# First token tile in two halves around the second one, its half sums kept in HBM, and every engine's queue in written order

## The chip, the cores and the metric

The kernel runs on one core of a Trainium2 chip. The metric is device time in microseconds of one execution; smaller is better. Engines are named as in the profile: PE (matmul), PEld (weight load), DVE (vector), ACT (scalar), POOL (GpSimd), SP (the queue that issues the DMAs).

## The reference

Attention within chunks of 64 tokens, then a feed-forward layer with g = h cos(h), all in fp32:

```python
scores = scale * np.matmul(q_c, k_c.transpose(0, 1, 2, 4, 3))      # chunk by chunk, 64 x 64
scores = scores - np.max(scores, axis=-1, keepdims=True)
attn = np.exp(scores)
attn = attn / (np.sum(attn, axis=-1, keepdims=True) + 1e-09)
out = np.matmul(attn, v_c)
...
x = out.transpose(0, 2, 1, 3).reshape(B * S, H * D)                 # 4608 x 512
h = x @ w_in                                                        # 512 -> 2048
g = h * np.cos(h)
return (g @ w_out).astype(np.float32)                               # 2048 -> 512
```

There are 8 batches, 8 heads, 576 tokens and a head size of 64. The weights arrive as 64-bit floats, so that the kernel turns them into fp32 itself.

## The kernel before

The 4608 tokens make NT = 9 tiles of TOK = 512. The hidden width of 2048 is cut into NFC = 16 chunks of 128. A step is one chunk of one tile: `hidden(t, fc)` is 12 matmuls into a bank `h` (four slices of x, each as high x high, high x low, low x high, since every fp32 operand is split into two fp32r parts), `activate` makes g and its parts `g_hi` and `g_lo`, and `project(t, fc)` is 12 matmuls that add to four banks `acc`, one for each 128 tokens (`sub`). `project` runs LAG = 3 steps behind `hidden`. After a tile's last chunk `finish` copies the four sums out and stores them.

`activate` alternates two engines: ACT L353 (multiples of 2 pi), DVE L354 (the remainder), ACT L356 (sine), DVE L357 (times h), ACT L360 (`g_hi`), DVE L361 (`g_lo`).

A weight block (`in` or `out`, 32 in all, 512 KB each) is decoded by `split_weight`: ACT L124 (Abs), L125 (Relu) and L126 build words of the fp32 number, DVE L127 adds the sign and L130 joins the words (called xor below), ACT L136 makes the high part and DVE L137 the low part. Tile 0 needs block after block; each is decoded once and kept.

Attention of a tile works on four pairs of heads (`hp`). For tiles 0 and 1 `scores_early` writes one bank per pair, `softmax` does the maximum, difference, exponential, sums, inverse and quotients (for tile 1 the quotients are one operation on POOL), `transposed` turns the weights on PE with a copy `pts` by ACT, and `weighted` multiplies with v and splits the result into the two parts of x (ACT L321, DVE L322). From tile 2 on `attend` spreads the same over the steps of the tile before, with DVE's 32x32 transposes, through small queues of closures (`soon`, `late`, `full`) that `activate` empties.

The order within an engine's queue is set by a scheduler for tile 0 and the start: `ordered` is False there, and the scheduler may move any instruction ahead of another. From tile 1 on `kept` holds the matmuls and most of the rest in written order. Blocks are decoded two steps ahead:

```python
AHEAD = 2
...
        if s + AHEAD < NFC:
            split_weight("in", s + AHEAD)
            split_weight("out", s + AHEAD)
```

Of the kernel before, what the change touches and what calls it, by code (L numbers as in the profile page):

```python
# [29 lines left out]
AHEAD = 2  # L30
# [10 lines left out]
def attention_then_cos_ffn(ctx: ExitStack, tc, qT, kT, v, w_in, w_out, out, wide):  # L41
# [17 lines left out]
    xp = ctx.enter_context(tc.tile_pool(name="xp", bufs=8))  # L59
    gp = ctx.enter_context(tc.tile_pool(name="gp", bufs=3))  # L60
    ps_o = ctx.enter_context(tc.tile_pool(name="ps_o", bufs=1, space=bass.MemoryType.PSUM))
# [15 lines left out]

    soon = deque()
    late = deque()
    full = deque()  # L80
# [30 lines left out]
    def split_weight(name, fc):  # L111

        raw, n = w_raw.pop((name, fc))
        w = dec.tile([P, n], F32, name="w")
        if not wide:
            nc.gpsimd.tensor_copy(w, raw[:, :n])
        else:
            top = raw[:, 4 : 4 + 4 * n].rearrange("p (n k) -> p n k", k=4)[:, :, 0]
            mid = raw.bitcast(U32)[:, 1 : 1 + 2 * n].rearrange("p (n k) -> p n k", k=2)[:, :, 0]


            half, low = half_words[(name == "out")], w.bitcast(U32)
            hb = half[:, :, 1]
            nc.scalar.activation(hb.bitcast(BF16), top.bitcast(BF16), AF.Abs)  # L124
            nc.scalar.activation(hb, hb, AF.Relu, bias=float(7 - (MORE << 7)), scale=8.0)  # L125
            nc.scalar.activation(low, mid, AF.Relu, bias=float((1 << 19) - 1), scale=-(2.0**-13))  # L126
            nc.vector.scalar_tensor_tensor(  # L127
                hb, top, 0x8000, hb, op0=ALU.bitwise_and, op1=ALU.bitwise_or
            )
            nc.vector.tensor_tensor(  # L130
                low, low, half.rearrange("p n k -> p (n k)").bitcast(U32), op=ALU.bitwise_xor
            )
        o = SHIFT if name == "in" else 0
        parts = wts.tile([P, 2 * n + PAD], F32R, name=f"w_{name}{fc}")
        hi, lo = parts[:, o : o + n], parts[:, o + n : o + 2 * n]
        nc.scalar.copy(out=hi, in_=w)  # L136
        nc.vector.tensor_tensor(lo, w, hi.bitcast(F32), op=ALU.subtract)  # L137
        w_parts[name, fc] = (hi, lo)
# [6 lines left out]
    probs = {}  # L145
    def load_qk(t, hp):
        qt, kt = (att.tile([P, TOK], F32, name=n, bufs=HP) for n in ("qt", "kt"))
        nc.sync.dma_start(out=qt, in_=qT[t, hp])
        nc.sync.dma_start(out=kt, in_=kT[t, hp])
        queries[t, hp] = (qt, kt)  # L150

    def load_v(t, hp):
# [3 lines left out]
        else:  # L156
            if hp == 2:
                values["roomy"] = xp.tile([P, 2, TOK], F32, name="x")
# [16 lines left out]
    def scores_early(t, hp, s):  # L175

        qt, kt = queries.pop((t, hp))
        for c in range(NCH):
# [6 lines left out]
        m = att.tile([P, NCH], F32, name="m", bufs=4)  # L185
        nc.vector.tensor_reduce(out=m, in_=sv, op=ALU.max, axis=AX.X)
        nc.vector.tensor_tensor(
            e[:, hp], sv, m.unsqueeze(2).broadcast_to([P, NCH, CH]), op=ALU.subtract
        )
# [30 lines left out]
    def softmax(t, a, b):  # L220

        n = (b - a) * NCH
        e = probs[t][:, a:b].rearrange("p a c k -> p (a c) k")
        nc.scalar.activation(e, e, AF.Exp, scale=SCALE)
        z = att.tile([P, HP * NCH], F32, name="z")
        zs = z[:, :n]
        nc.vector.tensor_reduce(out=zs, in_=e, op=ALU.add, axis=AX.X)
        nc.vector.tensor_scalar(zs, zs, 1e-9, None, op0=ALU.add)
        nc.vector.reciprocal(out=zs, in_=zs)

        eng = nc.gpsimd if t == 1 else nc.vector
        eng.tensor_tensor(e, e, zs.unsqueeze(2).broadcast_to([P, n, CH]), op=ALU.mult)

    def exponentials(t):
        e = probs[t].rearrange("p a c k -> p (a c k)")
        kept(nc.scalar.activation(e, e, AF.Exp, scale=SCALE))

    def divide(t):

        z = att.tile([P, HP, NCH], F32, name="z")  # L240

        def total(hp):
            kept(nc.vector.tensor_reduce(out=z[:, hp], in_=probs[t][:, hp], op=ALU.add, axis=AX.X))

        def inverse():
            kept(nc.vector.tensor_scalar(z, z, 1e-9, None, op0=ALU.add))
            kept(nc.vector.reciprocal(out=z, in_=z))

        def quotient(hp):
            e = probs[t][:, hp]  # L250
            zb = z[:, hp].unsqueeze(2).broadcast_to([P, NCH, CH])
            kept(nc.vector.tensor_tensor(e, e, zb, op=ALU.mult))

        soon.extend(lambda hp=hp: total(hp) for hp in range(HP))
        soon.append(inverse)
        return [lambda hp=hp: quotient(hp) for hp in range(HP)]

    def transposed(t, hp):
# [4 lines left out]
        pt = ps_h.tile([P, 512], F32, name="h") if t == 0 else bank("a", 0)  # L263
        for c in range(0, NCH, 2):
            nc.tensor.transpose(
# [3 lines left out]
            )  # L269
        nc.scalar.copy(out=pts, in_=pt)  # L270
# [19 lines left out]
    def weighted(t, hps, banks):  # L290
# [18 lines left out]
        if (t, g) not in x_parts:  # L309
            x_parts[t, g] = tuple(  # L310
                xp.tile([P, 2, TOK], F32R, name="x") for _ in range(2)
            )
        for par in range(2):
# [6 lines left out]
            def split(xq=xq, hi=hi, lo=lo):  # L320
                kept(nc.scalar.copy(out=hi, in_=xq))  # L321
                kept(nc.vector.tensor_tensor(lo, xq, hi.bitcast(F32), op=ALU.subtract))  # L322

            if t < EARLY:
                split()
            else:
                late.append(split)


    g_parts = {}  # L330
    acc = {}

    def hidden(t, fc):
        if t == 0 and fc in (2, 3):
            h = bank("a", fc)
        else:
            h = ps_h.tile([P, TOK], F32, name="h")
# [9 lines left out]
    def activate(t, fc, h):  # L347

        g = gp.tile([P, TOK], F32, name="g", bufs=2)
# [4 lines left out]
        kept(nc.vector.scalar_tensor_tensor(g, n, -2.0 * math.pi, h, op0=ALU.mult, op1=ALU.add))  # L354
        take(soon, 1)
        kept(nc.scalar.activation(g, g, AF.Sin, bias=0.5 * math.pi))  # L356
        kept(nc.vector.tensor_tensor(g, h, g, op=ALU.mult))  # L357
        take(soon, 1)
        take(full, 2)
        kept(nc.scalar.copy(out=g_hi, in_=g))  # L360
        kept(nc.vector.tensor_tensor(g_lo, g, g_hi.bitcast(F32), op=ALU.subtract))  # L361
        g_parts[t, fc] = (g_hi, g_lo)
# [3 lines left out]
    def project(t, fc):  # L366
        g_hi, g_lo = g_parts.pop((t, fc))
        w_hi, w_lo = w_parts["out", fc]
        for sub in range(NSUB):
            if fc == 0:  # L370
# [3 lines left out]
            matmul(o, g_hi[:, ss], w_hi, start=(fc == 0), stop=False)  # L374
            matmul(o, g_hi[:, ss], w_lo, start=False, stop=False)
            matmul(o, g_lo[:, ss], w_hi, start=False, stop=(fc == NFC - 1))
            if fc == NFC - 1:
                full.append(lambda sub=sub, o=o: finish(t, sub, o))

    def finish(t, sub, o):  # L380
        if t == NT - 1:
            if sub % 2 == 0:
                acc["last"] = xp.tile([P, 2, DM], F32, name="x")
            os = acc["last"][:, sub % 2]
        else:

            os = (wts if sub % 2 else dec).tile([P, DM], F32, name=f"half{sub // 2}" if sub % 2 else "w")
# [149 lines left out]
```

## Time and profile before

| | |
|---|---|
| median of 3 runs | 880.53 us (880.53 to 880.63) |
| the profiled execution | 880.95 us |
| its span, first to last instruction | 879.1 us |
| mean granted clock of PE | 0.986 |
| HBM read, written | 45.09 MB, 9.44 MB |
| DMA queue q1 | 17.7% of 16 engines |

Spans of the profile are counted from the first instruction. A group of matmuls shows its first start and its last end; the time from start to start of neighbours is what an operation costs on a queue that never waits, since its end overlaps with the next start. In brackets behind a row stands how long the engine idled ahead of it and who ended that.

### The profile page before, as it was taken

The numbers are of one execution on the slowest core, as the hardware profiler recorded it, in microseconds if no ns is written. First come the engines' busy times: TensorE is split into PE (matmuls) and PEld (weight loads), VectorE is DVE, ScalarE is ACT, GpSimd is POOL, SyncE is SP. The second block draws the span as 40 slices with busy tenths as digits, with TensorE's granted clock in tenths as the row PEclk, the third lists the DMA queues.
The fourth block names the chain that finished last, engine by engine and source line by source line (L and its number), as shares of the span: only waits on it lengthen the run. The fifth ranks groups of instructions, "written<-read, shape, count | busy, mean of one in ns | idle before, by whom it ended". The sixth has DMA issues, their size and how long they took to land.

```text
span 879.1 us, 14100 instructions
## 1 busy us (share of the span) xinstructions
PE 853.0 (97%) x5792; PEld 697.1 (79%) x5792; DVE 576.7 (66%) x975; ACT 407.9 (46%) x660; POOL 5.5 (1%) x9
## 2 busy tenths in 40 slices
PE   4899999999999999999999999999999999999998
PEld 3587777888888888888888888888888888888886
DVE  5999986766577656764686558655766577644332
ACT  4998993533354335333533344333533354333332
POOL 0001000000000000000000000000000000000000
PEclk8599999999999999999999999999999999999999
DMA  9980013100310012001300040003100010001001
GB/s 346 406 340 33 14 25 110 47 26 25 96 49 25 24 49 96 25 1 50 120 1 25 25 145 1 25 25 97 49 25 25 1 48 25 1 1 48 1 1 48
DMA packets 25407, 55.42 MB, mean 63 GB/s; under 512 B 2816, under 2 KB 2816, under 8 KB 25344
## 3 DMA queue, kind: packets, MB, share of 16 engines
q1 hardware_dynamic: 25344, 54.54, 17.7%
q8 instruction: 45, 0.74, 0.4%
q14 instruction: 18, 0.15, 0.1%
HBM read 45.09 MB, written 9.44 MB: 62 GB/s over the span
## 4 chain that ended last, share of the span: by engine, by line
PE 85%; ACT 11%; DMA 1%; DVE 1%; issue 1%; SPq 0%; ACTq 0%
PE acc L74 41%; PE h L74 40%; PE a L74 4%; ACT half L124 2%; ACT half L125 2%; ACT w L126 2%; DMA w_out<-in_w_out_dram 1%; ACT g_hi L360 1%; ACT g L356 1%; ACT w_out L136 1%; ACT w_in L136 1%; ACT g L353 1%; DMA kt<-in_kT_dram 1%; ACT pts L270 0%; ACT x L321 0%
## 5 line engine op out<-in xcount | busy, mean ns | idle before, releaser
L74 PE MATMUL h<-x,w_in 128*128 128x512 f32 x1704 | 416.9, 393 | 5.9 <-ACT x L321 2.8
L74 PEld LDWEIGHTS h<-x,w_in 128*128 128x128 f32 x1704 | 321.1, 189 | 75.0 <-DVE g L357 4.5
L74 PE MATMUL acc<-w_out,g_hi 128*128 128x512 f32 x1152 | 355.2, 392 | 0.0
L74 PEld LDWEIGHTS acc<-w_out,g_hi 128*128 128x128 f32 x1152 | 214.0, 188 | 45.2
L74 PE MATMUL acc<-w_out,g_lo 128*128 128x512 f32 x576 | 221.1, 390 | 0.6 <-DVE g_lo L361 0.6
L354 DVE SCALAR_TENSOR_TENSOR g<-g,h 128x512 f32<-128x512 int32 x142 | 97.2, 684 | 138.3 <-ACT g L353 137.6
L353 ACT ACTIVATE g<-h 128x512 int32<-128x512 f32 x142 | 84.7, 596 | 190.1 <-PE h L74 190.1
L361 DVE TENSOR_TENSOR g_lo<-g,g_hi 128x512 fp32r<-128x512 f32 x144 | 102.5, 712 | 79.9 <-ACT g_hi L360 77.0
L356 ACT ACTIVATE g<-g 128x512 f32<-128x512 f32 x144 | 91.0, 632 | 128.2 <-DVE g L354 128.0
L360 ACT CAST g_hi<-g 128x512 fp32r<-128x512 f32 x144 | 89.3, 620 | 128.9 <-DVE g L357 79.3
L357 DVE TENSOR_TENSOR g<-h,g 128x512 f32<-128x512 f32 x142 | 98.1, 691 | 56.5 <-ACT g L356 53.0
L74 PEld LDWEIGHTS acc<-w_out,g_lo 128*128 128x128 f32 x576 | 108.1, 188 | 23.7 <-DVE g_lo L361 1.1
L282 DVE STREAM_TRANSPOSE pts<-e 32x256 f32<-32x256 f32 x224 | 97.4, 435 | 3.7
L125 ACT ACTIVATE half<-half 128x512 uint16<-128x512 uint16 x32 | 25.1, 786 | 0.2
L74 PEld LDWEIGHTS a<-kt,qt 64*64 64x64 f32 x1024 | 18.9, 135 | 7.6 <-issue 6.8
L130 DVE TENSOR_TENSOR w<-w,half 128x512 uint32<-128x512 uint32 x32 | 22.0, 687 | 1.8 <-ACT w L126 1.0
L74 PEld LDWEIGHTS a<-pts,vt 64*64 64x64 f32 x1024 | 16.6, 134 | 7.2 <-issue 5.3
L322 DVE TENSOR_TENSOR x<-a,x 128x512 fp32r<-128x512 f32 (+1 forms) x38 | 21.9, 614 | 0.1
L74 PE MATMUL a<-kt,qt 64*64 64x64 f32 x1024 | 21.8, 222 | 0.0
L74 PE MATMUL a<-pts,vt 64*64 64x64 f32 x1024 | 19.0, 222 | 0.7 <-ACT pts L270 0.7
L216 DVE TENSOR_TENSOR e<-a,m 128x512 f32<-128x512 f32 x28 | 19.2, 686 | 0.5
L212 DVE TENSOR_REDUCE m<-a 128x8 f32<-128x512 f32 x28 | 19.2, 684 | 0.0
(61 smaller groups left out, 316.5 us busy)
## 6 DMA issues: line engine op xcount, KB each, us to landing
qt<-in_qT_dram SPq DMA_DIRECT2D x36, 256.0 KB, 4.0
kt<-in_kT_dram SPq DMA_DIRECT2D x36, 256.0 KB, 4.2
vt<-in_v_dram SPq DMA_DIRECT2D x34, 256.0 KB, 3.0
w_in<-in_w_in_dram SPq DMA_DIRECT2D x16, 512.0 KB, 9.1
w_out<-in_w_out_dram SPq DMA_DIRECT2D x16, 512.0 KB, 9.4
out_dram<-w SPq DMA_DIRECT2D x16, 256.0 KB, 2.1
out_dram<-half SPq DMA_DIRECT2D x16, 256.0 KB, 2.0
out_dram<-x SPq DMA_DIRECT2D x4, 256.0 KB, 2.0
```

Of the source, the lines that this page charges most:

```text
L74: kept(nc.tensor.matmul(*args, **kw))
L125: nc.scalar.activation(hb, hb, AF.Relu, bias=float(7 - (MORE << 7)), scale=8.0)
L130: nc.vector.tensor_tensor(low, low, half.rearrange("p n k -> p (n k)").bitcast(U32), op=ALU.bitwise_xor)
L212: kept(nc.vector.tensor_reduce(out=m, in_=sv, op=ALU.max, axis=AX.X))
L282: kept(nc.vector.transpose(out=dst[o : o + BL, :, qb], in_=src[i : i + BL, :, kb]))
L322: kept(nc.vector.tensor_tensor(lo, xq, hi.bitcast(F32), op=ALU.subtract))
L353: kept(nc.scalar.activation(n, h, AF.Identity, bias=0.25, scale=0.5 / math.pi))
L354: kept(nc.vector.scalar_tensor_tensor(g, n, -2.0 * math.pi, h, op0=ALU.mult, op1=ALU.add))
L356: kept(nc.scalar.activation(g, g, AF.Sin, bias=0.5 * math.pi))
L357: kept(nc.vector.tensor_tensor(g, h, g, op=ALU.mult))
L360: kept(nc.scalar.copy(out=g_hi, in_=g))
L361: kept(nc.vector.tensor_tensor(g_lo, g, g_hi.bitcast(F32), op=ALU.subtract))
```

## The change

The steps are taken in another sequence: tile 0's chunks 0 to 7 (GROUP = 8), all 16 chunks of tile 1, tile 0's chunks 8 to 15, then tiles 2 to 8 as before. At the end of the first half the four sums of tile 0 go to HBM (`partial`); they are loaded again in step 28, by `resume`, and DVE adds them to the second half's sums in step 34. Tile 1's attention, which had all 16 steps of tile 0, now has eight.

The 32 blocks are decoded over 19 steps: two at the start (`in` 0 and 1, where four were), then one or two inside each `activate` (`split_in`), for the first eight chunks two steps ahead of their use, for the others in turn until step 18. Three pieces of a block stand between the operations of the activation, so that the sequence on each engine is written out. `ordered` is gone: every instruction of ACT, DVE and PE keeps the written order from the first on. The start is written out by hand too; two of tile 0's quotients go to POOL, and tile 1's are four operations there. The buffers `xp` are half as many under two names.

```diff
+GROUP = 8
...
-    ordered = False
-
     def kept(ins):
-        if ordered:
-            tc.keep_in_program_order(ins)
+        tc.keep_in_program_order(ins)
         return ins
...
+    order = [(0, fc) for fc in range(GROUP)] + [(1, fc) for fc in range(NFC)]
+    order += [(t, fc) for t in range(NT) if t != 1 for fc in range(0 if t else GROUP, NFC)]
...
+    partial = [hbm.tile([P, DM], F32, name=f"partial{sub}") for sub in range(NSUB)]
...
-    def activate(t, fc, h):
+    left = []
+    def activate(t, fc, h, blocks=()):
+        nothing = [lambda: None] * 7
+        one, two = ([split_weight(*b) for b in blocks] + [nothing, nothing])[:2]
...
         kept(nc.scalar.activation(n, h, AF.Identity, bias=0.25, scale=0.5 / math.pi))
         kept(nc.vector.scalar_tensor_tensor(g, n, -2.0 * math.pi, h, op0=ALU.mult, op1=ALU.add))
+        for piece in left:
+            piece()
+        left.clear()
+        for piece in one[:2]:
+            piece()
         take(soon, 1)
         kept(nc.scalar.activation(g, g, AF.Sin, bias=0.5 * math.pi))
+        for piece in one[2:4]:
+            piece()
         kept(nc.vector.tensor_tensor(g, h, g, op=ALU.mult))
+        one[4]()
         take(soon, 1)
+        take(urgent, len(urgent))
         take(full, 2)
         kept(nc.scalar.copy(out=g_hi, in_=g))
+        two[0]()
         kept(nc.vector.tensor_tensor(g_lo, g, g_hi.bitcast(F32), op=ALU.subtract))
+        for piece in one[5:] + two[1:5]:
+            piece()
+        left.extend(two[5:])
...
+    def resume():
+        for sub in range(NSUB):
+            os = acc["partial", sub] = out_room(sub)
+            nc.sync.dma_start(out=os, in_=partial[sub])
...
+        if half == 0 and step in (1, 2):
+            for hp in (2 * step - 2, 2 * step - 1):
+                late.append(scores_early(t, hp, bank("a", hp)))
+        if half == 0 and step == 3:
+            late.append(lambda: exponentials(t))
+        if half == 0 and step == 4:
+            soon.extend(lambda hp=hp: total(t, hp) for hp in range(HP))
+            soon.append(lambda: inverse(t))
+            soon.extend(lambda hp=hp: quotient(t, hp, nc.gpsimd) for hp in range(HP))
+        hp = {(5, 1): 0, (6, 0): 1, (7, 0): 2, (7, 1): 3}.get((step, half))
+        if hp is not None:
+            take(late, len(late))
+            (late if hp < HP - 1 else urgent).extend(weighted(t, (hp,), (bank("a", 0), bank("a", 1))))
...
+        if (step, half) in ((5, 0), (6, 1)):
+            take(late, len(late))
+            for hp in range(2 * (step - 5), 2 * (step - 4)):
+                transposed(t, hp)
...
+    for fc in range(2, GROUP):
+        split_in.setdefault(fc - 2, []).append(("in", fc))
+    for fc in range(GROUP - 1):
+        split_in.setdefault(fc + 1, []).append(("out", fc))
+    rest = [("out", GROUP - 1)] + [(k, fc) for fc in range(GROUP, NFC) for k in ("in", "out")]
+    s = GROUP
+    while rest:
+        k = 1 + (s % 2 == 0)
+        split_in[s], rest = rest[:k], rest[k:]
+        s += 1
```

The line numbers of the operations move: L353, L354, L356, L357, L360, L361 become L370, L371, L378, L381, L386, L388; L124 to L126 become L136 to L138, L127 and L130 become L140 and L143, L136 and L137 become L150 and L155. Below, `half` names belong to decode, `a` banks to attention.

On ACT, where tile 1's first turned weights (`pts`) are copied, before:

```order
L353 ACTIVATE g<-h 128x512
L136 CAST w_out_991<-w 128x512
L124 ACTIVATE half_89<-w_out_176 128x512
L360 CAST g_hi<-g 128x512
L125 ACTIVATE half_89<-half_89 128x512
L356 ACTIVATE g<-g 128x512
L136 CAST w_in_1034<-w 128x512
L124 ACTIVATE half_87<-w_in_178 128x512
L270 COPY pts<-a_797 128x512
L126 ACTIVATE w<-w_out_176 128x512
```

and now, from the end of step 4 into step 5:

```order
L386 CAST g_hi<-g 128x512
L136 ACTIVATE half_91<-w_out_158 128x512
L150 CAST w_in_733<-w 128x512
L137 ACTIVATE half_91<-half_91 128x512
L138 ACTIVATE w<-w_out_158 128x512
L281 COPY pts<-a_763 128x512
L281 COPY pts<-a_770 128x512
L370 ACTIVATE g<-h 128x512
L150 CAST w_out_815<-w 128x512
L136 ACTIVATE half_89<-w_in_164 128x512
```

One copy among decode and the activations of two steps has become two copies ahead of everything of step 5.

On DVE, the sums and inverse of tile 1's softmax (`z`), which the quotients on POOL wait for, before:

```order
L361 TENSOR_TENSOR g_lo<-g,g_hi 128x512
L127 SCALAR_TENSOR_TENSOR half_87<-w_in_170,half_87 128x512
L228 TENSOR_SCALAR z<-z 128x32
L137 TENSOR_TENSOR w_out_908<-w,w_out_908 128x512
L357 TENSOR_TENSOR g<-h,g 128x512
L130 TENSOR_TENSOR w<-w,half_87 128x512
L229 RECIPROCAL z<-z 128x32
```

and now, in step 4:

```order
L388 TENSOR_TENSOR g_lo<-g,g_hi 128x512
L155 TENSOR_TENSOR w_in_733<-w,w_in_733 128x512
L140 SCALAR_TENSOR_TENSOR half_91<-w_out_158,half_91 128x512
L143 TENSOR_TENSOR w<-w,half_91 128x512
L257 TENSOR_REDUCE z<-e 128x8 x2
L261 TENSOR_SCALAR z<-z 128x32
L262 RECIPROCAL z<-z 128x32
L371 SCALAR_TENSOR_TENSOR g<-g,h 128x512
```

The sums, which were one operation ahead of these rows, are four in step 4, and the last two and the inverse stand behind the step's decode.

On DVE at the change from step 1 to step 2, where tile 1's scores are taken from their banks, now:

```order
L140 SCALAR_TENSOR_TENSOR half_91<-w_out_126,half_91 128x512
L143 TENSOR_TENSOR w<-w,half_91 128x512
L212 TENSOR_REDUCE m<-a_484 128x8
L214 TENSOR_TENSOR e<-a_484,m 128x512
L212 TENSOR_REDUCE m<-a_502 128x8
L214 TENSOR_TENSOR e<-a_502,m 128x512
L371 SCALAR_TENSOR_TENSOR g<-g,h 128x512
```

The four operations stand together ahead of the next step's L371, where those of the third and fourth pair were spread before:

```order
L186 TENSOR_REDUCE m<-a_602 128x8
L137 TENSOR_TENSOR w_in_847<-w,w_in_847 128x512
L130 TENSOR_TENSOR w<-w,half_89 128x512
L186 TENSOR_REDUCE m<-a_662 128x8
L357 TENSOR_TENSOR g<-h,g 128x512
L187 TENSOR_TENSOR e<-a_602,m 128x512
L127 SCALAR_TENSOR_TENSOR half_87<-w_in_166,half_87 128x512
L354 SCALAR_TENSOR_TENSOR g<-g,h 128x512
L187 TENSOR_TENSOR e<-a_662,m 128x512
```

On SP's queue four stores of `partial` come after tile 2's first v loads, and its four loads among tile 1's output stores.

More of the change, by code (lines that the diff above doesn't have):

```diff
@@ L268, in transposed @@
                 identity=ident,
[L269 to L270 removed]
+            ))
+        kept(nc.scalar.copy(out=pts, in_=pt))
         probs[t, hp] = pts
@@ L364, in activate, with project @@
             take(queue, len(queue))
-    def project(t, fc):
+    def project(s):
+        t, fc = order[s]
+        first = s == 0 or order[s - 1][0] != t
+        last = s == len(order) - 1 or order[s + 1][0] != t
         g_hi, g_lo = g_parts.pop((t, fc))
@@ new lines, in attention_then_cos_ffn @@
+        if fc == 3:
+            prefetch(1)
+    for fc in (NFC - 2, NFC - 1):
+        load_weight("out", fc)
+    blocks = [("in", fc) for fc in range(2)]
+    w0, w1 = (split_weight(*b) for b in blocks)
+    below = [scores_early(0, hp, bank("acc", hp)) for hp in range(HP)]
+    below[0]()
+    exponentials(0, 0, 1)
+    below[1]()
+    exponentials(0, 1, 2)
+    total(0, 0)
+    below[2]()
+    exponentials(0, 2, 3)
+    total(0, 1)
+    inverse(0, 0, 2)
+    quotient(0, 0, nc.gpsimd)
+    quotient(0, 1, nc.gpsimd)
@@ new lines, in attention_then_cos_ffn @@
+    w0[0]()
+    below[3]()
+    exponentials(0, 3, 4)
+    total(0, 2)
+    for piece in w0[1:5]:
+        piece()
+    total(0, 3)
+    inverse(0, 2, 4)
+    quotient(0, 2)
+    quotient(0, 3)
+    transposed(0, 0)
+    x0 = weighted(0, (0,), (bank("a", 0), bank("a", 1)))
+    transposed(0, 1)
+    x1 = weighted(0, (1,), (bank("acc", 0), bank("acc", 1)))
+    for piece in x0 + w0[5:]:
+        piece()
+    transposed(0, 2)
+    transposed(0, 3)
+    x2 = weighted(0, (2,), (bank("acc", 2), bank("acc", 3)))
```

250 lines of the change are left out of this document (125 added, 125 removed).

## The prediction

> **What bounds the kernel now.** I read the page's first block, the table by windows, the chain that ended last, then the timeline where the bound changes.
>
> ```profile
> PE 853.0 (97%) x5792; PEld 697.1 (79%) x5792; DVE 576.7 (66%) x975; ACT 407.9 (46%) x660; POOL 5.5 (1%) x9
> ```
> ```profile
> 10.00:20.00 10.00, 3.18 (x61) 2.43 (x56) 8.63 (x17) 6.73 (x12) 0.00 (x0) 0.79 1.04 409
> 20.00:30.00 10.00, 5.99 (x94) 4.10 (x90) 9.02 (x21) 9.97 (x21) 0.00 (x0) 0.50 1.04 401
> 30.00:40.00 10.00, 7.98 (x75) 5.19 (x74) 8.86 (x16) 9.97 (x20) 0.00 (x0) 0.67 1.02 406
> ...
> 100.00:110.00 10.00, 10.00 (x47) 8.09 (x46) 9.10 (x16) 10.00 (x19) 0.00 (x0) 1.00 0.01 3
> ...
> 200.00:300.00 100.00, 100.00 (x675) 82.23 (x674) 65.40 (x114) 39.38 (x62) 0.00 (x0) 1.00 0.13 43
> ```
> The columns are PE, PEld, DVE, ACT, POOL, granted clock, DMA share. From 200 us on PE is full and ACT at 39%: PE-bound. From 20 to 110 ACT is full; PE's "full" there is stretched, since far fewer matmuls fit.
>
> ```profile
> 230.26 2.95 PE acc L74 x12
> ...
> 322.58 2.95 PE acc L74 x12
> ...
> 446.37 2.72 PE h L74 x12
> ...
> 864.69 10.89 PE acc L74 x48
> ```
> Twelve matmuls, which are one `hidden` or one `project`, take 2.72 us. A tile repeats after 322.58 - 230.26 = 92.32 us; 32 x 2.72 = 87.04 of it is the feed-forward, so 5.28 is attention. PE ends at 864.69 + 10.89 = 875.58. Counting back: tiles 1 to 8 need 128 `hidden` and 131 `project` (three are left over from tile 0 by LAG), 259 x 2.72 = 704.5, and seven attentions 37.0. So tile 1 begins at 134.1, and from there nothing is lost. All that can change lies ahead of 134.1, where tile 0 is held by ACT's decode.
>
> **ACT's price list** comes from a stretch in which it never idles; what counts is start to start.
>
> ```profile
> 94.59 0.59 ACT L360 CAST g_hi<-g 128x512 fp32r<-128x512 f32 x1
> ...
> 95.09 0.59 ACT L353 ACTIVATE g<-h 128x512 int32<-128x512 f32 x1
> 95.41 0.67 DVE L361 TENSOR_TENSOR g_lo<-g,g_hi 128x512 fp32r<-128x512 f32 x1
> ...
> 95.58 0.68 ACT L126 ACTIVATE w<-w_in 128x512 uint32<-128x512 uint32 x1
> 96.01 0.67 DVE L354 SCALAR_TENSOR_TENSOR g<-g,h 128x512 f32<-128x512 int32 x1
> ...
> 96.16 0.61 ACT L136 CAST w_out<-w 128x512 fp32r<-128x512 f32 x1
> ...
> 96.67 0.80 ACT L124 ACTIVATE half<-w_out 128x512 bf16<-128x512 bf16 x1
> ...
> 97.32 0.61 ACT L356 ACTIVATE g<-g 128x512 f32<-128x512 f32 x1
> 97.83 0.79 ACT L125 ACTIVATE half<-half 128x512 uint16<-128x512 uint16 x1
> ...
> 98.47 0.62 ACT L136 CAST w_in<-w 128x512 fp32r<-128x512 f32 x1
> ...
> 99.62 0.36 ACT L321 CAST x<-a 128x256 fp32r<-128x256 f32 x1
> 99.87 0.68 ACT L126 ACTIVATE w<-w_out 128x512 uint32<-128x512 uint32 x1
> ```
> The first number of a row is its start. A decode block costs ACT 0.65 (L124) + 0.64 (L125) + 0.57 (L126) + 0.50 (L136) = 2.36; a step's activation 0.49 (L353) + 0.51 (L356) + 0.50 (L360) = 1.50; half a split of x (L321) 0.25. DVE takes 0.60 for an operation of 128x512.
>
> ```profile
> 42.57 0.83 ACT L124 ACTIVATE half<-w_in 128x512 bf16<-128x512 bf16 x1
> ...
> 43.43 0.79 ACT L125 ACTIVATE half<-half 128x512 uint16<-128x512 uint16 x1
> ...
> 70.84 1.28 ACT L224 ACT_TABLE_LOAD   x1
> ...
> 72.14 1.92 ACT L224 ACTIVATE e<-e 128x2048 f32<-128x2048 f32 x1
> ...
> 73.96 0.64 ACT L126 ACTIVATE w<-w_out 128x512 uint32<-128x512 uint32 x1
> ...
> 82.81 3.89 POOL L232 TENSOR_TENSOR e<-e,z 128x2048 f32<-128x2048 f32 x1 [80.63 <-ACT w L126]
> ...
> 133.19 0.57 ACT L270 COPY pts<-a 128x512 f32<-128x512 f32 x1
> 133.32 0.69 DVE L357 TENSOR_TENSOR g<-h,g 128x512 f32<-128x512 f32 x1 [0.70 <-ACT g L356]
> ...
> 134.05 0.62 ACT L360 CAST g_hi<-g 128x512 fp32r<-128x512 f32 x1 [0.28 <-DVE g L357]
> ```
> The first pair is Abs with its Relu right behind it: 0.86 instead of 0.65, so 0.2 is lost. A table load costs 1.30, the large exponential 1.82, one quarter of POOL's quotients 0.97. The last rows show a chain from DVE's product to `g_hi`: 0.69 and 0.04 until ACT starts.
>
> **The start.** DVE begins as now:
>
> ```profile
> 6.35 0.69 DVE L186 TENSOR_REDUCE m<-acc 128x8 f32<-128x512 f32 x1 [6.35 <-PE acc L74]
> ...
> 24.56 1.08 PE L265 MATMUL h<-ident,e 128*128 128x128 f32 x4 [1.48 <-DVE e L232]
> ...
> 27.60 1.13 PE L74 MATMUL a<-pts,x 64*64 64x64 f32 x32
> ...
> 41.58 0.62 ACT L353 ACTIVATE g<-h 128x512 int32<-128x512 f32 x1
> ```
> Its new queue up to the last quotient: four maxima and subtractions 5.3, three sums 1.8 and the last 0.6, two inversions 0.9, two operations of one decode 1.5, one quotient 0.6, and 1.6 of waits for ACT: 18.6. From there two transposes, a copy and a `weighted` at half clock, and the last halves of x behind a decode in ACT's queue, 8.8: 27.4. Six matmuls of the first `hidden` are left, at half clock 2.7, and 0.5 of latencies: it ends at 30.6. Now the first activation follows at 41.58, but with eight blocks decoded; then it will be two. The 11 us are no gain by themselves, since 6 x 2.36 = 14.2 of ACT's work is owed.
>
> **Steps 0 to 7** (tile 0's half, with all of tile 1's attention). ACT's work: 8 x 1.50 = 12.0; 13 blocks x 2.36 = 30.7; tile 1: three table loads 3.9, exponential 1.8, four `pts` copies 1.9, eight splits 2.0. Together 52.3. PE's own, 13 x 2.72 = 35.4 and some 7 of attention, lies beside it. Then the waits of a queue in written order, which I laid out row by row at the prices above:
> - g_hi stands behind Sin and only one decode operation; Sin 0.6 and the product 0.7 (begun behind L140) are not covered: 0.3 to 0.8 in seven steps, 3.7. Abs to Relu, 8 x 0.2 = 1.5. High parts that wait for DVE's xor, 1.8.
> - In steps 1 and 2 four DVE operations of tile 1's scores (4 x 0.65) stand ahead of the next step's L371, so Sin is late by 1.3 each: 2.6.
> - In step 5 two `pts` copies stand ahead of the step's first activation. They wait for the transposes, these for POOL's quotients, these for the inversion behind the last two sums on DVE. Counted from ACT's last operation of step 4: the rest of DVE's decode 1.3, two sums 1.2, inversion 0.5, quotient 0.97, transposes 0.6 make 4.6, and the second copy waits 0.5. In step 6 the other two copies wait 1.8 for `project`.
> - `hidden` 8 needs all of tile 1's x, whose last quarter is handled in step 7: 2.0.
> Sum 18.4. ACT starts at 30.7; 30.7 + 52.3 + 18.4 = 101.4, and the ninth `hidden` ends at about 101.
>
> **From there.** 135 `hidden` and 139 `project`: 274 x 2.72 = 745.3; attention 37.0. Decode goes on with 17 blocks in 11 steps: 11 x 1.50 + 17 x 2.36 = 56.6 against PE's 11 x 5.44 = 59.8, so PE leads, but with ACT and DVE about 4 us behind it, and three PE waits are left: tile 1's first `project` for the banks, whose last two copies stand behind decode, 2.5; tile 2's second pair of scores for banks that DVE empties at the end of its step (2 x 1.9 of decode and four operations, 2.4, beside 1.8 of its own), 5.8; its first `weighted` for DVE's 32x32 transposes, late after the exponential's 4.4, 2.5. Together 10.8. If LAG covers them it is nothing: that is the lower end.
>
> The parked sums (four stores, four loads of 256 KB) cost nothing: loads are issued in step 28 and used in step 34, six steps or 32 us later, and a landing takes:
>
> ```profile
> out_dram<-w SPq DMA_DIRECT2D x16, 256.0 KB, 2.1
> ```
> On SP's queue they pass only loads that are wanted steps later. Four adds on DVE in place of two copies add 1.2 where DVE is at 65%: nothing.
>
> Sum: 101 + 745.3 + 37.0 + 10.8 = 894.1. After PE's end come 879.1 - 875.6 = 3.5, around the span 880.95 - 879.1 = 1.85: 899.5 for a profiled execution, which stands 0.4 above the median: **899 us**.
>
> [...]
>
> **Rivals.**
> *ACT stays as full as now* (faster). Other work slips into every gap and the waits vanish: 30.7 + 52.3 = 83.0, then 745.3 + 37.0 + 5.3: 870. For it: ACT is at 9.97 of 10 from 20 us on. Against: there a decode operation fills each gap, in the new order the gap's next instruction is the waiting one. It decides from the point where under 11 of the 29 us of waits come. Chance 0.11.
> *The PE clock drops in the gaps.* PE gets pauses of 5 us (step 2) and 12 us (ahead of the transposes in step 5). In the trace:
>
> ```profile
> 12.50:15.00 2.50, 0.00 (x0) 0.00 (x0) 2.36 (x4) 0.51 (x2) 0.00 (x0) 1.00 1.01 407
> 15.00:17.50 2.50, 0.00 (x0) 0.00 (x0) 2.50 (x7) 1.80 (x4) 0.00 (x0) 0.67 1.02 418
> 17.50:20.00 2.50, 1.96 (x36) 1.56 (x36) 2.50 (x5) 2.50 (x5) 0.00 (x0) 0.50 1.04 402
> ```
> Without matmuls for some 5 us the clock went to 0.50. At half clock `project`, `weighted` and `hidden` between that pause and step 6 take 2.7 + 0.7 + 2.7 = 6.1 more, of which ACT's own work in step 5 covers some 2, and the `hidden` after the pause in step 2 takes 2.7 more: about 7, so 906. Chance 0.22. [...]
> *LAG covers the later waits*: 888. Chance 0.15.
> *No change that can be measured* (two thirds of the waits covered): 0.04.
> The forecast itself: 0.48, with a range of 892 to 903 of its own.
>
> **How the numbers follow.** Slower 0.48 + 0.22 + 0.15 = 0.85; same 0.04, within 0.2%, about what a measurement of this kernel can tell; faster 0.11. The range takes in the three slower cases with some room for waits missed, 882 to 911.
>
> **What would show it.** Right: the first activation near 31; ACT idle ahead of the first `pts` copies of tile 1 for about 5 us, released by PE; the ninth `hidden` ending near 101; then a PE that is full but for three waits of 2 to 6 us between 115 and 205; steps from 210 on as now. Wrong: an ACT at 9.9 of 10 from 31 to 85, or a ninth `hidden` that ends before 90.

## The result, and the profile after

The changed kernel takes 908.17 us (median; 906.77 to 909.43), the kernel before 880.58 beside it: 1.0307 times as long, with a 95% interval of 1.0285 to 1.0329. It is 3% slower, where the forecast had 2%; the forecast of 899.0 was 9.2 us too low, inside its range of 882 to 911. The profiled execution took 907.83, its span 906.1. Medians and ratios here and below are of fast runs; one run of the "sums ahead" kernel, in a slow state at 3002.38 us, is left out.

The page's engines and its row of granted clocks:

```profile
PE 859.4 (95%) x5792; PEld 701.8 (77%) x5792; DVE 579.4 (64%) x976; ACT 412.6 (46%) x660; POOL 7.7 (1%) x14
...
PEclk8887999899999999999999999999999999999999
```

The matmuls are the same; PE's share fell from 97 to 95% of a longer span, and the clock is not full in several of the first eight slices (each 22.7 us). The table by windows says where (PE, PEld, DVE, ACT, POOL, granted clock, DMA share). First the kernel before at 70 us:

```profile
70.00:80.00 10.00, 10.00 (x46) 8.29 (x45) 9.36 (x14) 9.95 (x14) 0.00 (x0) 1.00 0.00 0
```

and the changed kernel:

```profile
70.00:80.00 10.00, 4.10 (x15) 3.39 (x16) 5.21 (x10) 4.33 (x9) 4.04 (x4) 0.54 0.00 0
...
160.00:170.00 10.00, 8.27 (x81) 6.94 (x82) 6.79 (x12) 4.24 (x7) 0.00 (x0) 0.66 0.33 105
...
250.00:300.00 50.00, 50.00 (x338) 40.98 (x337) 37.01 (x64) 20.48 (x30) 0.00 (x0) 1.00 0.20 64
```

ACT, at 9.95 of 10 before, is busy 4.33 of 10 at 70 us, with PE at 4.10 and DVE at 5.21: they wait for each other. From 250 us on nothing is lost. ACT's timeline shows the waits, and PE's row behind it the longest pause:

```profile
29.56 0.59 ACT L370 ACTIVATE g<-h 128x512 int32<-128x512 f32 x1
...
46.36 0.63 ACT L378 ACTIVATE g<-g 128x512 f32<-128x512 f32 x1 [1.21 <-DVE g L371]
...
77.05 0.58 ACT L281 COPY pts<-a 128x512 f32<-128x512 f32 x1 [5.26 <-PE a L276]
...
87.98 0.65 ACT L331 CAST x<-a 128x256 fp32r<-128x256 f32 x2 [1.89 <-PE a L73]
...
91.45 1.07 ACT L281 COPY pts<-a 128x512 f32<-128x512 f32 x2 [2.82 <-PE a L276]
...
103.63 0.60 ACT L370 ACTIVATE g<-h 128x512 int32<-128x512 f32 x1 [0.84 <-PE h L73]
```
```profile
75.90 2.12 PE L276 MATMUL a<-ident,e 128*128 128x128 f32 x8 [13.38 <-POOL e L267]
```

L370, L378 and L386 are now the activation's three ACT operations (L353, L356, L360 before), L371 and L381 DVE's, L281 the copy of turned weights, L331 half a split of x, L276 the transposes. ACT's last row is the ninth activation, the first of tile 1; I call its start the ninth activation below. PE's waits behind it, and its twelves in the chain that ended last:

```profile
122.94 0.74 PE L73 MATMUL acc<-w_out,g_hi 128*128 128x512 f32 x2 [1.36 <-ACT pts L434]
124.12 0.73 PE L73 MATMUL acc<-w_out,g_hi 128*128 128x512 f32 x2 [0.21 <-DVE vt L436]
...
157.48 0.30 PE L73 MATMUL a<-kt,qt 64*64 64x64 f32 x2 [1.12 <-issue]
161.73 1.98 PE L73 MATMUL a<-kt,qt 64*64 64x64 f32 x62 [3.96 <-DVE e L243]
...
207.35 0.68 PE L73 MATMUL a<-pts,vt 64*64 64x64 f32 x28 [2.48 <-DVE pts L293]
```
```profile
163.71 4.90 PE acc L73 x12
...
208.04 4.54 PE acc L73 x12
...
302.22 2.95 PE acc L73 x12
...
394.71 2.95 PE acc L73 x12
...
891.52 10.98 PE acc L73 x48
```

The three waits are those that the prediction named. Behind the last two of them one `project` takes 4.90 and 4.54 in place of 2.72: half clock (granted 0.50 in 162 to 166 and in 210 to 212). PE ends at 902.50, against 875.58 before.

### The profile page after: what moved, and what is told of

It is laid out like the page before. It is cut to its first block, busy times and chain, and to the rows that moved or that the text cites. A ratio compares the mean times of both kernels' runs of the same rounds, so it can differ in the third digit from the quotient of the medians.

```text
span 906.1 us, 14142 instructions
## 1 busy us (share of the span) xinstructions
PE 859.4 (95%) x5792; PEld 701.8 (77%) x5792; DVE 579.4 (64%) x976; ACT 412.6 (46%) x660; POOL 7.7 (1%) x14
## 4 chain that ended last, share of the span: by engine, by line
PE 79%; ACT 11%; DVE 8%; issue 1%; DMA 1%; SPq 0%; POOL 0%; ACTq 0%; DVEq 0%; POOLq 0%
PE acc L73 39%; PE h L73 36%; PE a L73 4%; ACT half L137 2%; ACT half L136 2%; DVE half L140 2%; ACT g_hi L386 1%; DVE g L381 1%; DVE w L143 1%; ACT w_in L150 1%; ACT g L370 1%; ACT w_out L150 1%; DVE pts L293 1%; ACT g L378 1%; DMA kt<-in_kT_dram 1%
## 5 line engine op out<-in xcount | busy, mean ns | idle before, releaser
L73 PE MATMUL acc<-w_out,g_hi 128*128 128x512 f32 x1152 | 362.5, 396 | 1.6 <-ACT pts L434 1.4
L73 PE MATMUL acc<-w_out,g_lo 128*128 128x512 f32 x576 | 226.4, 393 | 0.0
L371 DVE SCALAR_TENSOR_TENSOR g<-g,h 128x512 f32<-128x512 int32 x144 | 98.6, 684 | 145.8 <-ACT g L370 145.1
L370 ACT ACTIVATE g<-h 128x512 int32<-128x512 f32 x144 | 85.8, 596 | 187.2 <-PE h L73 187.0
L388 DVE TENSOR_TENSOR g_lo<-g,g_hi 128x512 fp32r<-128x512 f32 x144 | 99.7, 693 | 81.1 <-ACT g_hi L386 76.5
L386 ACT CAST g_hi<-g 128x512 fp32r<-128x512 f32 x144 | 89.4, 621 | 136.3 <-DVE g L381 83.8
L378 ACT ACTIVATE g<-g 128x512 f32<-128x512 f32 x144 | 90.7, 630 | 128.3 <-DVE g L371 128.2
L381 DVE TENSOR_TENSOR g<-h,g 128x512 f32<-128x512 f32 x144 | 99.4, 690 | 55.0 <-ACT g L378 51.7
L73 PEld LDWEIGHTS a<-kt,qt 64*64 64x64 f32 x1024 | 20.8, 145 | 16.6 <-issue 16.6
L73 PEld LDWEIGHTS a<-pts,vt 64*64 64x64 f32 x1056 | 18.1, 137 | 13.7 <-issue 4.9
L73 PE MATMUL a<-pts,vt 64*64 64x64 f32 x1056 | 21.1, 225 | 6.4 <-DVE x L334 2.7
L137 ACT ACTIVATE half<-half 128x512 uint16<-128x512 uint16 x32 | 25.1, 783 | 0.6
L257 DVE TENSOR_REDUCE z<-e 128x8 f32<-128x512 f32 x36 | 23.7, 678 | 0.0
L143 DVE TENSOR_TENSOR w<-w,half 128x512 uint32<-128x512 uint32 x32 | 22.0, 688 | 1.3
L250 ACT ACTIVATE e<-e 128x2048 f32<-128x2048 f32 (+1 forms) x12 | 17.9, 1488 | 10.2 <-DVE e L214 10.1
```

Source lines behind the costliest of these rows:

```text
L73: kept(nc.tensor.matmul(*args, **kw))
L137: lambda: kept(nc.scalar.activation(hb, hb, AF.Relu, bias=more, scale=8.0)),
L143: lambda: kept(nc.vector.tensor_tensor(*[w().bitcast(U32)] * 2, words, op=ALU.bitwise_xor)),
L257: kept(nc.vector.tensor_reduce(out=sums[t][:, hp], in_=probs[t][:, hp], op=ALU.add, axis=AX.X))
L370: kept(nc.scalar.activation(n, h, AF.Identity, bias=0.25, scale=0.5 / math.pi))
```

## The experiments

| kernel | median us | ratio to before (95%) | ninth activation | PE end |
|---|---|---|---|---|
| changed | 908.17 | 1.0307 (1.0285 to 1.0329) | 103.63 | 902.50 |
| free order | 901.12 | 1.0219 (1.0203 to 1.0236) | 114.91 | 895.30 |
| written order, no split | 910.91 | 1.0330 (1.0312 to 1.0348) | | 904.49 |
| turned weights behind activation | 907.01 | 1.0289 (1.0268 to 1.0310) | 102.67 | 901.22 |
| tile 2's scores later | 899.25 | 1.0201 (1.0182 to 1.0221) | 103.82 | 895.66 |
| sums ahead | 904.83 | 1.0270 (1.0253 to 1.0288) | 101.50 | 898.92 |
| rewritten | 881.50 | 1.0004 (0.9995 to 1.0014) | 90.37 | 875.95 |
| rewritten, free order | 895.21 | 1.0163 (1.0148 to 1.0179) | 110.84 | 891.59 |
| rewritten, a step earlier | 882.89 | 1.0022 (1.0013 to 1.0031) | 91.34 | 876.85 |
| and `out` blocks later | 884.86 | 1.0041 (1.0027 to 1.0054) | 91.34 | 878.77 |
| quotients on DVE | 881.75 | 1.0005 (0.9997 to 1.0014) | 91.33 | 876.89 |
| and scores in steps 0, 2 | 882.31 | 1.0012 (1.0004 to 1.0021) | 91.28 | 876.82 |
| `project` first | 879.73 | 0.9987 (0.9978 to 0.9996) | 88.57 | 874.13 |

My theory was that the written order makes the loss, wait by wait; its rivals, that the split does, or that a written order costs a fixed amount per step.

**Free order.** The change, with the scheduler free until step 19:

```diff
     def kept(ins):
-        tc.keep_in_program_order(ins)
+        if ordered:                      # s >= 19
+            tc.keep_in_program_order(ins)
```

> The changed kernel, but until step 19 the scheduler may move instructions of ACT, DVE and PE, as in the kernel before; the split of tile 0, the spread of the decode and the parked sums stay. Theory (the written order makes the loss): of the roughly 21 us in which ACT waits between its first activation at 29.6 and the end of the ninth `hidden` at 103.6, most goes, since decode that is ready fills the gaps; the ninth `hidden` ends at 84 to 90, the PE pauses near 157 and 205 shrink, and the time is 870 to 885. Rival (squeezing tile 1's attention into eight steps makes the loss, whoever orders it): the chain from the last sums over POOL's quotients to the turned weights is as long as before, the ninth `hidden` ends at 98 or later, and the time stays at 900 to 910.

901.12: 7 us of 27 come back, so the theory missed. Both of the rival's numbers came (a ninth `hidden` at 98 or later, 900 to 910): tile 1's attention is what the next tile waits for here too, and its chain is longer than in the written order, not only as long (ACT's eighth and ninth activation, then windows):

```profile
89.55 0.59 ACT L373 ACTIVATE g<-h 128x512 int32<-128x512 f32 x1
114.91 0.57 ACT L373 ACTIVATE g<-h 128x512 int32<-128x512 f32 x1
```
```profile
100.00:110.00 10.00, 6.16 (x71) 4.39 (x70) 8.26 (x15) 10.00 (x21) 0.00 (x0) 0.71 0.15 56
110.00:120.00 10.00, 7.46 (x73) 5.36 (x72) 9.12 (x16) 9.97 (x19) 0.00 (x0) 0.50 0.57 173
```

Tile 0's eight steps are done by 90, earlier than in the written order, but tile 1's x is not there. ACT is full of decode that no step needs yet, and the hand-overs of tile 1's attention (`weighted`, split, turned weights, `weighted`) queue behind it. The ninth activation is 11 us later than in the changed kernel, and the spread of the decode is lost. Behind it little is lost, one PE wait of 3.47: from 114.91 to PE's end are 780.4 us, in the changed kernel 798.9.

**Written order, no split.**

```diff
-GROUP = 8
+GROUP = 16
...                # and no partial sums, no resume
```

> The written order alone: tile 0 keeps its 16 steps in one piece, two blocks are decoded in each of them, nothing is parked in HBM; every queue keeps the written order. Theory (the written order makes the loss): an ACT step is 1.50 + 2 x 2.36 = 6.2 of work and 1.2 or so of waits, so that tile 1 begins 16 to 24 us later than the 134.1 of the kernel before, and the time is 896 to 906, near the changed kernel or a little under it, since the split buys little that the waits don't take back. Rival (the split makes the loss): about 880 to 885, as before.

910.91, above the range of the theory (896 to 906): this written order costs 30 us without the split. It isn't the order alone, though. The code keeps tile 1's attention in steps 1 to 7, where sixteen steps are there for it, and PE waits 12.95 us for POOL's quotients as in the changed kernel. Behind that stand two-block steps without tile 1's attention (activations):

```profile
122.71 0.57 ACT L370 ACTIVATE g<-h 128x512 int32<-128x512 f32 x1
130.35 0.58 ACT L370 ACTIVATE g<-h 128x512 int32<-128x512 f32 x1
...
163.76 0.59 ACT L370 ACTIVATE g<-h 128x512 int32<-128x512 f32 x1
```

A step takes 7.64 for 1.50 + 2 x 2.36 = 6.22 of ACT's work; before, eight steps from 81.58 to 131.21 took 6.20 each. The seventeenth activation comes at 163.76, where the first of tile 1 came at 136.94 before. So each version loses by itself (30 us the written order without the split, 20 the split in free order), and the two together lose no more than the larger.

**Two moves of one wait.** First the copies, and with them the first two rounds of `weighted`, half a step later; then the sums:

```diff
-        hp = {(5, 1): 0, (6, 0): 1, (7, 0): 2, (7, 1): 3}.get((step, half))
+        hp = {(6, 0): 0, (6, 1): 1, (7, 0): 2, (7, 1): 3}.get((step, half))
...
-        if (step, half) in ((5, 0), (6, 1)):     # transposes and pts copies
+        if (step, half) in ((5, 2), (6, 2)):     # 2: behind the activation
```

> One wait moved: tile 1's transposes and their `pts` copies are written behind the activation of steps 5 and 6, not ahead of it, so that the 5.3 us in which ACT waits for POOL's quotients at 72 to 77 us pass beside an activation. Theory (each wait of ACT in the first eight steps is paid in full): the ninth `hidden` ends 4 to 6 us earlier and the time falls by as much, to 902 to 904. Rival (the wait only moves: the later turned weights make the later `weighted` and tile 1's x late instead): less than 1.5 us, 907 to 909.

907.01: the rival. The 5.26 us are gone, and other waits stand in their place:

```profile
78.44 0.62 ACT L386 CAST g_hi<-g 128x512 fp32r<-128x512 f32 x1 [2.13 <-PE a L276]
...
96.14 0.65 ACT L331 CAST x<-a 128x256 fp32r<-128x256 f32 x2 [4.30 <-PE a L73]
...
102.67 0.60 ACT L370 ACTIVATE g<-h 128x512 int32<-128x512 f32 x1 [1.26 <-PE h L73]
```

```diff
-            soon.extend(total ...); soon.append(inverse); soon.extend(quotient ...)
+            first.extend(total ...); first.append(inverse); first.extend(quotient ...)
     # activate(): first is emptied right behind DVE's first operation
```

> One thing moved in the changed kernel: in step 4 the four sums of tile 1, their inversion and POOL's quotients are written directly behind the first DVE operation of the activation, not spread between the decode of that step. In the changed kernel DVE idles 2.66 us ahead of that operation, and the last two sums come at 72.9 us. Theory (the sums' place sets the 5.3 us wait of ACT in step 5): the quotients start near 68 instead of 74.8, ACT's wait for the turned weights goes, and the time falls by 3 to 5, to 903 to 905. Rival (what follows, two banks handed from `weighted` to the next turned weights and back, sets the end of tile 1's attention, as moving the copies alone left the time at 907.0): ACT's wait goes and others grow in steps 6 and 7, 906 to 908.

904.83, at the upper end of the theory (903 to 905), though the trace has the rival's mechanism in it too. The copies no longer wait, step 5 begins 4.45 earlier (74.08, not 78.53), but half of that goes to the second pair:

```profile
73.60 0.59 ACT L282 COPY pts<-a 128x512 f32<-128x512 f32 x1
74.08 0.61 ACT L371 ACTIVATE g<-h 128x512 int32<-128x512 f32 x1
...
89.35 1.08 ACT L282 COPY pts<-a 128x512 f32<-128x512 f32 x2 [4.36 <-PE a L277]
```

What holds steps 5 to 7 is the chain of tile 1's attention, not one wait of it.

**Tile 2's scores later.**

```diff
-                attend(to, step)
+                if to > 2 or step == 0:
+                    attend(to, step)
+                elif step > 1:
+                    attend(to, step - 1)
```

> One PE wait moved: tile 2's second pair of scores and the attention steps behind them are issued one step later, when DVE has emptied the banks. Theory (the PE pause at 157 to 162 us is paid with the half clock behind it): 6.3 us of waiting and 2.1 of half clock go, `project` after it takes 2.72 again, and the time falls by 6 to 9, to 899 to 902. Rival 1 (LAG or DVE's queue lets PE wait elsewhere): tile 2's first `weighted` becomes later by what was won, less than 3 us in all, 905 to 908. Rival 2 (the clock drop is not tied to the pause): 6 us go, and a `project` of 4.8 stays.

899.25: 8.9 us less, the theory (PE at the same place):

```profile
159.13 2.88 PE L73 MATMUL h<-x,w_in 128*128 128x512 f32 x12
161.95 1.22 PE L73 MATMUL a<-kt,qt 64*64 64x64 f32 x64
```

The scores start without a wait, take 1.22 for 64 where the changed kernel's 62 took 1.98, and no `project` near them is stretched. The ninth activation is where it was (103.82). The wait, 5.1, and its half clock, 2.2 + 0.8, make 8.1. From the ninth activation to PE's end the trace is 7.0 shorter (798.9 became 791.8), with one new PE wait of 1.04 at 183.51; the medians differ by 8.9, between runs that spread over some 2.5 us. So the wait and its half clock were paid, nearly in full.

**Rewritten.** All at once, in written order: sums ahead; `weighted` in two rounds of two pairs; the second block's Abs ahead of `g_hi`; tile 1's maxima and differences between the decode operations; tile 2's attention later.

```diff
+        two[0]()
         kept(nc.scalar.copy(out=g_hi, in_=g))
-        two[0]()
...
-        hp = {(5, 1): 0, (6, 0): 1, (7, 0): 2, (7, 1): 3}.get((step, half))
+        if half == 1 and step in (5, 6):
+            hps = (2 * step - 10, 2 * step - 9)
+            urgent.extend(weighted(t, hps, (bank("a", 0), bank("a", 1))))
...
+    later = {0: (0,), 10: (8, 9)}      # tile 2: the other steps one later
```

> Written order throughout, five places rewritten: tile 1's sums directly behind the first DVE operation of step 4; tile 1's `weighted` in two rounds of two pairs (steps 5 and 6) in place of four rounds of one; the second block's Abs ahead of the `g_hi` copy; tile 1's maxima and differences between the decode operations, not behind them; tile 2's attention a step later from its second scores on, its first `weighted` two steps later. Theory (the loss is the waits that the written order holds, place by place): the ninth `hidden` ends near 88 to 92 instead of 103.6, the PE pauses near 157 and 205 go, and the time is 878 to 888. Rival (the written order costs a fixed amount in every step, wherever the operations stand): the first eight steps still take 8 us or more each, the ninth `hidden` ends at 97 or later, and only the two PE pauses go: 893 to 898.

881.50, the theory; the ninth activation at 90.37, 13.3 earlier, and PE ends at 875.95:

```profile
85.46 0.60 ACT L381 ACTIVATE g<-h 128x512 int32<-128x512 f32 x1
90.37 0.60 ACT L381 ACTIVATE g<-h 128x512 int32<-128x512 f32 x1 [0.18 <-PE h L73]
```

Of the 26.7 us that this wins over the changed kernel, 13.3 lie ahead of the ninth activation and 13.3 behind it (798.9 became 785.6). So the loss lay in where the rows stand, and in four rounds of `weighted` where two do. Only two of the five places were tried by themselves, the sums (3.3 us) and tile 2's attention (8.9); how the rest divides among the others is not shown.

**Rewritten, free order.** The same code with the scheduler free until step 19.

> The same code as the rewritten version, with the scheduler free to move instructions until step 19. Theory (in the free order decode that is ready goes ahead of tile 1's attention on ACT and DVE, so each hand-over of that chain costs more): ACT is full until about 120, tile 1's x is late though the chain has two rounds fewer, the ninth `hidden` ends at 103 to 112, and the time is 887 to 897, slower than the written version. Rival (the free order fills the gaps and the shorter chain is all it needed): 870 to 880, faster than the written version.

895.21, the theory; the eighth and the ninth activation:

```profile
91.75 0.59 ACT L384 ACTIVATE g<-h 128x512 int32<-128x512 f32 x1
110.84 0.60 ACT L384 ACTIVATE g<-h 128x512 int32<-128x512 f32 x1 [0.53 <-PE h L76]
```

So for the rewritten code this scheduler is 13.7 us worse than the written order, while for the changed kernel's code it was 7.1 better: neither order is the better one by itself. The 30 us by which the kernel before beats the unsplit written order are no third case, since those two differ in tile 1's attention as well.

**Four attempts to go on.** They end within 3.4 us of the rewritten version, none faster. A step earlier (`step in (0, 1)` for the scores, the rest of tile 1's attention a step earlier too, and its sums now ahead of the activation's first DVE operation):

> The rewritten version with tile 1's attention a step earlier throughout (scores in steps 0 and 1, exponential at the end of step 2, sums in step 3 ahead of that step's first DVE operation, turned weights in steps 4 and 5). Theory (in the rewritten version the ninth `hidden` waits for ACT's and DVE's work alone, whose idle places left are DVE at 30 to 35 us and PE's waits for the scores' banks at 39 to 46 us): the DVE idle time at 30 to 35 is used, step 2 loses the 2.8 us it had over its ACT work, and the ninth activation comes at 87 to 89 instead of 90.4: 878 to 880. Rival (the same waits stand one step earlier): within 1 us of the rewritten version's 881.5.

882.89, 1.4 slower than the rewritten version, and so 0.4 beyond the rival's margin: `hidden` is now late behind the scores, and PE waits for the quotients as before.

```profile
44.55 0.60 ACT L381 ACTIVATE g<-h 128x512 int32<-128x512 f32 x1 [2.20 <-PE h L73]
```

Then `out` blocks one step later (`split_in[fc + 2]`, not `fc + 1`), ahead of the step's `in` block:

> The version before this one, and each of the first eight `out` blocks decoded one step later, ahead of the step's `in` block, so that one block less (2.36 us of ACT, 1.9 of DVE) lies in the first eight steps and 18 instead of 17 behind them. Theory (the first eight steps are ACT's and DVE's work, and PE leads behind them): the ninth activation comes 2 to 3 us earlier and the time falls by as much, to 875 to 878. Rival 1 (PE waits for the later `out` parts in each `project`, so that the next `hidden` is late): no gain or a loss of up to 4 us. Rival 2 (behind the eighth step ACT can't carry the eighteenth block): what is won is given back there, within 1 us of the version before.

884.86, the first rival, though not only by the `out` parts that it named: ACT has 2.36 less to do ahead of the ninth activation, and that comes no earlier, since PE waits for parts that are decoded just in time, longest for an `in` part, which now stands behind an `out` block.

```profile
57.37 0.96 PE L73 MATMUL h<-x,w_in 128*128 128x512 f32 x3 [3.13 <-DVE w_in L156]
...
91.34 0.60 ACT L381 ACTIVATE g<-h 128x512 int32<-128x512 f32 x1 [1.78 <-PE h L73]
```

Quotients on DVE (`quotient(t, hp)` in place of `quotient(t, hp, nc.gpsimd)`), and with them scores in steps 0 and 2:

> The rewritten version with tile 1's four quotients on DVE in place of POOL. In the rewritten version, while POOL's four quotients run (5.64 us, against 4.04 in the changed kernel, where DVE stood idle), DVE's decode operations beside them take 1.53 to 1.58 us in place of 0.68. Theory (POOL and DVE hold each other up there, and the four slowed operations cost DVE about 3): the four quotients cost DVE 4 x 0.6 = 2.4, the slowed operations take 0.68 again, ACT's waits of 1.25, 0.16 and 1.07 in steps 4 and 5 shrink, and the time falls by 0.5 to 2: 879.5 to 881. Rival (DVE is the fuller engine in those steps, and 2.4 us of work put on it is paid): slower by 1 to 2, 882.5 to 883.5.

> The version with the quotients on DVE, and tile 1's scores in steps 0 and 2 in place of 1 and 2, so that each pair finds its banks empty and half of the maxima and differences lie in DVE's idle time at 30 to 35 us. Theory (the first eight steps are held by these waits: PE for the banks at 39 to 46 us with a half-clock `hidden` behind it, ACT 0.87, 0.54 and 0.80): step 2 loses some 2 us, the ninth activation comes near 87 to 88, and the time is 877 to 879, faster than the kernel before. Rival (as when all of tile 1's attention was moved a step ahead: the waits find another place, since q and k of tile 1 or step 0's empty DVE slots come too late): within 1 us of the version with the quotients on DVE alone.

881.75 and 882.31: no gain from either; the first lies between theory and rival, the second is the rival. In all of these but the one with `out` blocks later, PE waits in front of tile 1's first transposes (here the rewritten version, with the first matmuls of the `project` behind the wait, which takes 4.90 in place of 2.72, mean granted clock 0.77 in 60 to 70; then the quotients on DVE):

```profile
65.69 1.11 PE L287 MATMUL a<-ident,e 128*128 128x128 f32 x4 [4.87 <-POOL e L278]
...
67.93 1.20 PE L73 MATMUL acc<-w_out,g_hi 128*128 128x512 f32 x2
```
```profile
65.77 1.09 PE L287 MATMUL a<-ident,e 128*128 128x128 f32 x4 [4.34 <-DVE e L278]
```

**`project` first.** That order turned round in step 5. A second edit went with it: tile 1's sums stand ahead of step 4's first DVE operation, as in the version a step earlier, and the inversion goes with the first quotient:

```diff
-        if half == 0 and step in (5, 6):         # transposes
+        if (step, half) in ((5, 1), (6, 0)):     # in step 5 behind project
```

> The version with the quotients on DVE, and in step 5 `project` of step 2 written ahead of the first two turned weights on PE, with tile 1's sums ahead of step 4's first DVE operation. In the four versions near 881 us PE waits 4.3 to 6.5 us for tile 1's first quotient in front of the first transposes, with a ready `project` queued behind them, and that `project` then takes 4.0 to 5.0 us at half clock in place of 2.72; from 70 us on PE never idles until 109. Theory (this pause is what holds all of them near 881, whatever ACT and DVE won before it): `project` fills 2.7 us of the pause, the half clock behind it shrinks, ACT's wait for `weighted` in step 5 (1.38) and for the ninth `hidden` (0.73) go, and the time is 877.5 to 879.5, 0.15 to 0.4% faster than the kernel before. Rival (ACT's work in steps 5 to 8 sets the ninth activation, as its few waits there suggest): within 1 us of 881.7.

879.73, 2.0 less than with the quotients on DVE (which of the two edits brought it is not shown) and 0.13% less than the kernel before (0.04 to 0.22%), about as little as a measurement can tell: the theory's direction, at the small end; 879.73 is 0.2 above its range.

```profile
61.16 0.51 PE L73 MATMUL acc<-w_out,g_hi 128*128 128x512 f32 x1 [0.78 <-ACT w_out L151]
63.88 0.50 PE L73 MATMUL acc<-w_out,g_hi 128*128 128x512 f32 x1 [2.21 <-DVE w_out L156]
...
68.09 1.04 PE L287 MATMUL a<-ident,e 128*128 128x128 f32 x8
...
88.57 0.60 ACT L381 ACTIVATE g<-h 128x512 int32<-128x512 f32 x1 [0.29 <-PE h L73]
```

The transposes no longer wait, but `project` does, for its low part, which now stands behind the sums on DVE; with that 2.21 gone there might be a little more. That was not tried.

## Why the prediction was right, and where its sizes were off

- *The start*: first activation forecast at 30.7, measured at 29.56. Right: the 11 us were no gain.
- *Steps 0 to 7*: the ninth `hidden` was forecast to end at about 101; the ninth activation begins at 103.63. From 29.56 that is 74.1, so beside the 52.3 of work ACT lost 21.8, not 18.4 (the list adds up to 18.5). Its main items were there: Sin 1.21 and 1.11 (1.3 each forecast), step 5's copies 5.26 + 0.41 (4.6 + 0.5), step 6's 2.82 (1.8). One was not on the list: ACT's wait of 1.89 at 87.98 for the second `weighted`, which waited for DVE's split of the first. Others came out smaller (`g_hi` 2.9 for 3.7, the last quarter of x 0.84 for 2.0), so that the named waits make 19.0; this nearness is in part luck. The other 2.8 no row names.
- *PE's three waits*: 1.36 + 0.21, 1.12 + 3.96 and 2.48 make 9.1; 2.5, 5.8 and 2.5 were forecast. (The terms given for the 5.8 add up to 8.0; what was taken off is not said.) The rival that LAG covers them is refuted for the largest by the shifted scores (8.9 us).
- *The mis-sized term* is PE behind its waits. The sum took 2.72 for every `project`; two took 4.90 and 4.54, 4.0 together, and the scores 0.8 more. The rival of the dropping clock (906) had the mechanism, but put all of it, 8.8 us less what ACT covers, in steps 2 to 6. There I count some 2.7 (64 scores 3.68 where step 0's took 2.08, a `hidden` 2.98, a `project` 3.54); the 4.8 stood behind tile 2's waits, where PE is the bound. That its 906 is nearer to 908.17 than my 899 is luck. The half clock came behind a pause of 2.48 us (granted 0.50 in 210 to 212), and behind one of 2.46 at the same place in the kernel with tile 2's scores later (4.54 again, granted 0.50 in 208 to 210); behind one of 2.27 in the unsplit kernel it did not come (2.90, granted 1.00 in 170 to 180).
- *The period*: 394.71 - 302.22 = 92.49, against 92.32; seven times, 1.2. Together: 2.6 - 1.7 + 4.0 + 0.8 + 1.2 = 6.9 of the 8.4 by which PE ended later than forecast; 1.5 I can't assign.
- *Table loads*: the exponential or sine starts 1.29 to 1.30 behind each of the three loads, as the sum has it (1.30); nothing more shows in the rows.
- *Parked sums and adds*: nothing, as forecast, beside PE's first wait of 1.57, which is for their copies. The loads landed 3.5 to 3.7 us after issue, not 2.1 (that row was of a store), still far less than the 32 us there are; PE is at 37.00 of 37 from 213 to 250 us and at 50.00 of 50 from 250 on.
- *ACT stays as full as now* (870): refuted by ACT at 4.33 of 10. Its premise, that work which slips into gaps would make the split pay, is refuted too: in the free order the split lost 20 us.

## What to carry to other kernels

A split that frees the bound engine pays only if what it waits for next is ready: here tile 1's attention had eight steps in place of sixteen, and both orders were late with it, the free one because decode that nobody needed yet went first, the written one because the next row of a queue was the waiting one. To mend a written order, look for a ready operation queued behind a waiting one, on every engine of the chain; within that chain, moving one wait alone mostly moved it on (1.2 and 3.3 us of 5.3), while five places together gave 26.7. Where PE was the bound, the longest of its waits cost its length and the half clock behind it (5.1 and 3.0 us), and moving it alone paid.

## What the runs showed of the hardware

POOL's quotients and three of DVE's operations beside them took longer than apart. With the sums ahead POOL's quotients ran beside DVE's decode (POOL's row, then DVE's):

```profile
67.73 5.63 POOL L268 TENSOR_TENSOR e<-e,z 128x512 f32<-128x512 f32 x4 [52.42 <-DVE z L263]
```
```profile
68.03 1.57 DVE L141 SCALAR_TENSOR_TENSOR half<-w_in,half 128x512 uint16<-128x512 uint16 x1
69.50 0.67 DVE L383 TENSOR_TENSOR g<-h,g 128x512 f32<-128x512 f32 x1
...
70.94 1.53 DVE L390 TENSOR_TENSOR g_lo<-g,g_hi 128x512 fp32r<-128x512 f32 x1
72.39 1.53 DVE L156 TENSOR_TENSOR w_in<-w,w_in 128x512 fp32r<-128x512 f32 x1
```

The four take 5.63; in the changed kernel, with DVE idle beside them (4.53 us), 4.04. Three of DVE's operations (L141, L390, L156) take 1.53 to 1.57; with the quotients on DVE the same three take 0.69 to 0.74. The product L383 takes 0.67 here and 0.68 there; why it is spared the runs do not show.

In the changed kernel the clock also dropped after a pause was over. Behind the 2.48 us that ended at 207.35 (windows of the changed kernel, granted clock in the third column from the end):

```profile
206.00:208.00 2.00, 0.65 (x29) 0.58 (x29) 1.94 (x4) 0.17 (x1) 0.00 (x0) 1.00 0.37 116
208.00:210.00 2.00, 2.00 (x9) 1.59 (x8) 0.71 (x2) 0.63 (x1) 0.00 (x0) 0.71 0.42 90
210.00:212.00 2.00, 2.00 (x6) 1.63 (x5) 0.00 (x0) 0.00 (x0) 0.00 (x0) 0.50 0.11 41
```

PE was busy again for all of 208 to 212, and only there did the clock fall, to 0.71 and 0.50.
